# The last query rows' scores of a head pair as four 64x64 products, with the decay bias added outside the array

## The chip, the cores and the metric

The kernel runs on one core of one Trainium2 chip. The metric is device time in microseconds of one execution. PE is TensorE (the matrix engine; PEld its weight loads), DVE is VectorE, ACT is ScalarE, POOL is GpSimd, and SP is the engine whose queue issues most transfers.

## The reference

Attention over 4 batches, 8 heads, 576 positions and 64 dimensions, with a causal mask and a decay from the running sum of a gate, and behind it two feed-forward layers of 512 x 2048 x 512 with different activations on all 2304 tokens. The weights arrive as float64; the kernel splits each into two float32r parts and so runs three products for one in the layers.

```python
def _attn_ref(q, k, v, s):
    scale = 1.0 / np.sqrt(D)
    scores = scale * np.matmul(q, k.transpose(0, 1, 3, 2))
    causal = np.triu(np.ones((S, S), dtype=bool), k=1)
    cum = np.cumsum(np.maximum(s, 0.0), axis=-1)
    bias = -(cum[:, :, :, None] - cum[:, :, None, :])
    scores = np.where(causal, -1000000000.0, scores + np.minimum(bias, 0.0))
    scores = scores - np.max(scores, axis=-1, keepdims=True)
    attn = np.exp(scores)
    attn = attn / (np.sum(attn, axis=-1, keepdims=True) + 1e-09)
    return np.matmul(attn, v)
...
x = attention output as [2304, 512]
h = x @ w_in;  x = np.maximum(0.01 * h, h) @ w_out
h = x @ w_in;  x = (np.maximum(h, 0.0) + np.log1p(np.exp(-np.abs(h)))) @ w_out
```

## The kernel before

**Phases.** Attention comes first and lasts to about 250 us; from then on (the main part) the two layers run as one list of steps, in which a first product fills a bank `ps_h` in PSUM (line 143) and second products fill banks `ps_out` (line 709). Part of layer 0 is drawn into the attention phase: the class `Fill` puts six products of 512 columns (half of an `h` or `o` unit, lines 143 and 583) into each step, as soon as the tokens of a batch are there.

**Pairs, units, steps.** Attention treats two heads at a time (a pair, 16 in all). A pair has four units, in this order: the query rows 384 to 511 of each head (512 keys), the *last* unit with the 64 rows behind 512 of both heads (576 keys), rows 256 to 383, and the two tiles of the first 256 rows. The loop runs over steps n, one per unit; it is a pipeline written out by hand, and each engine's queue follows the order of the code. In step n the scores of unit n + 1 are issued to PE, unit n gets its maxima (DVE, line 305, one instruction that scales, masks and reduces, from PSUM to SBUF) and exponentials (ACT, line 319), unit n - 1 its divisors (DVE, 325 and 326) and normalization (POOL, line 330), and unit n - 2 its transposes (PE, lines 338, 342 and 347) and their copies out of PSUM (lines 359 and 361). The products with V (line 378) are issued in the steps i = 0 and i = 2 of the next pair.

**The scores.** Queries and keys lie in SBUF with the two heads of a pair on the two halves of the partitions. A tile of an ordinary unit is, for each head, a float32 product of 64 rows (`Q`, `K`, line 286, each of two passes in the trace) and a second product that adds the decay: `BQ` and `BK` hold the running sums in two float32r parts and rows of ones, so that their product is the difference of sums between key and query. The last unit (line 276) puts both heads' 64 queries side by side as 128 columns of a stationary operand that has zeros where the other head's dimensions are, and runs over each half of the keys with all 128 rows: `Q` times `K`, then `BQ` times `BK`. Pair 0 uses `BQ0` and `BK0`, built in float32 from the first scans, instead.

**PSUM.** In the attention phase one pool has banks by tag: `s0` and `s1` for scores (two each), `t` for transposes (two), `a` for the products with V and the wake-up (one), `m` for the fill (one). When the attention is over, this pool is closed, and two others are opened over the same space: five banks for `ps_out` and three for `ps_h`.

**Transfers.** In step i = 0 of a pair SP issues the next pair's Q and K and the rows of `BQ` and `BK` (five transfers, line 80, from the DRAM tile `bb_d`), in step i = 3 the next pair's V; weights (`rawi`, `rawo`) and stores of layer 0's partial sums lie in between. At the start, Q and K of pair 0 go through ACT's queue.

Of the kernel before, what the change touches and what calls it, by code (L numbers as in the profile page):

```python
# [2 lines left out]

# [27 lines left out]
def attn_moe_moe(ctx, tc, q, k, v, s, w1i, w1o, w2i, w2o, out):  # L31
# [18 lines left out]
    def pool(name, bufs=1, **kw):  # L50
        return tc.tile_pool(name=name, bufs=bufs, **kw)
# [6 lines left out]
    xh = keep.tile([P, KD, NT], F32R, tag="xh", name="xh")  # L58
    xl = keep.tile([P, KD, NT], F32R, tag="xl", name="xl")
    bb_d = dram.tile([B * H, 2, S], F32R, tag="bb_d", name="bb_d")  # L60
    part = dram.tile([B - 1, P, KD, FW], F32, tag="part", name="part")


# [6 lines left out]
    def tick():  # L70
        clock[0] += 1
        for fn, args in todo.pop(clock[0], ()):
            fn(*args)
# [5 lines left out]
    def move(dst, src, queue=nc.sync):  # L79
        queue.dma_start(dst.bitcast(F32), src.bitcast(F32))  # L80
# [72 lines left out]
    def attention(att, ps, fills):  # L153
# [1 line left out]

        ZQ = NB * P + 2 * TL
        own = [[slice(0, NB * P + TL)], [slice(0, NB * P), slice(NB * P + TL, ZQ)]]
        two = lambda nm, shape, dt=F32: [att.tile(shape, dt, tag=f"{nm}{i}", name=f"{nm}{i}") for i in range(2)]  # L160
        Q, K = two("Q", [P, ZQ]), two("K", [P, S])
        BQ, BK = two("BQ", [P, ZQ], F32R), two("BK", [P, S], F32R)
        V = two("V", [P, NB + 1, 2, D])

        PA = att.tile([P, 2, NB, P + TL], F32, tag="PA", name="PA")
# [10 lines left out]
        def blank(i):  # L176

            bq = BQ[i].bitcast(F32)
            nc.gpsimd.memset(bq, 0.0)
            for j in range(2):  # L180
                for c in own[j]:
                    nc.gpsimd.memset(bq[j * D:j * D + 2, c], 1.0)

        def wake(x):

            pt = ps.tile([P, 512], F32, tag="a", name="pt_w", bufs=1)
            for i in range(8):
                nc.tensor.matmul(pt[:, :P], x, x, start=True, stop=True)

        def decay0():  # L190

            pitch = list(s1.ap[0])[0]
            nc.sync.dma_start(
                bass.AP(s1.tensor, s1.offset, [[D * pitch, 2], [1, S]]), bass.AP(s.tensor, s.offset, [[S, 2], [1, S]])
            )
            load(0, "q", nc.scalar)
            nc.sync.dma_start(c0, s.rearrange("b h s -> (b h) s"))
            load(0, "k", nc.scalar)
            nc.vector.memset(one[:, :P], 1.0)
            wake(one[:, :P])  # L200
            nc.vector.memset(one[:, P:], 1.0)
            nc.vector.memset(base, 0.0)
            for j in range(2):
                nc.vector.memset(base[j * D + 32:j * D + 33], -1.0)
            for i in (1, 0):
                nc.vector.memset(BK[i].bitcast(F32), -1.0)
            nc.vector.tensor_scalar(s0[:1], s1[:1], 0.0, 1.0 / scale, op0=ALU.max, op1=ALU.mult)
            for y, x in ((s0[D:D + 1], s1[D:D + 1]), (c0, c0)):
                nc.scalar.activation(y, x, AF.Relu, scale=1.0 / scale)
            nc.vector.tensor_tensor_scan(BK0, one, s0, base, op0=ALU.mult, op1=ALU.add)  # L210
            nc.scalar.activation(BQ0[32:33, :S], BK0[:1], AF.Copy)
            n = 0
            for c, queue in zip(own[1], (nc.vector, nc.gpsimd)):
                m = n + c.stop - c.start
                queue.tensor_copy(BQ0[D + 32:D + 33, c], BK0[D:D + 1, n:m])
                n = m

        hi, lo = one[:BH], c0

# [4 lines left out]
        def parts():  # L224
            nc.vector.tensor_tensor(lo.bitcast(F32R), c1, hi, op=ALU.subtract)
            for e, x in enumerate((hi, lo)):
                nc.sync.dma_start(bb_d[:, e, :].bitcast(F32), x)

        def zeros():
            nc.gpsimd.memset(PZ[TL:], 0.0)  # L230
# [2 lines left out]
            b, hp = divmod(p, NPAIR)  # L233
            return b, slice(2 * hp, 2 * hp + 2)

        def load(p, nm, queue=nc.sync):
            if p < NP:
                t, x = {"q": (Q, q), "k": (K, k), "v": (V, v)}[nm]
                queue.dma_start(t[p % 2], x[p])

        def rows(p):

            if p < NP:
                b, hs = heads(p)
                for j in range(2):
                    h, r = b * H + hs.start + j, j * D
                    move(BK[p % 2][r:r + 2], bb_d[h])
                    n = 0
                    for c in own[j]:
                        m = n + c.stop - c.start  # L250
                        move(BQ[p % 2][r + 32:r + 34, c], bb_d[h, :, n:m])
                        n = m


        class Unit:
            def __init__(self, p, ts):
                self.p, self.ts = p, ts
                self.last = not ts
                o = 0
                self.subs = []  # L260
                for t in ts:
                    self.subs.append((t, slice(o, o + (t + 1) * P)))
                    o += (t + 1) * P
                self.W = S // 2 if self.last else o
                self.n = 1 if self.last else 2 * len(ts)

            def scores(self):
                i = self.p % 2
                bq, bk = (BQ[i], BK[i]) if self.p else (BQ0, BK0)
                ops = (Q[i], K[i]), (bq, bk)  # L270
                self.ps = [ps.tile([P, 512], F32, tag=f"s{j}", name="pt_s", bufs=2) for j in range(2)]
                if self.last:

                    for j, pt in enumerate(self.ps):
                        for x, y in ops:
                            nc.tensor.matmul(  # L276
                                pt[:, :self.W], x[:, NB * P:], y[:, j * self.W:(j + 1) * self.W],
                                start=x is Q[i], stop=x is bq,
                            )
# [14 lines left out]
            def maxima(self, j):  # L294
                if j == 0:
# [2 lines left out]
                    if self.last:  # L298
                        self.sc = view(self.sc, 0, [self.W, 2], [1, self.W])
                w = slice(0, self.W)  # L300
                todo = [(w, (mask[:, w], maskl)[j], j)] if self.last else [
                    (c, mask[:, (NB - 1 - t) * P:], j * len(self.subs) + i) for i, (t, c) in enumerate(self.subs)
                ]
                for c, m, e in todo:
# [117 lines left out]
            blank(i)  # L422
        decay()
        fill.step(-2)
        load(1, "q")
        load(1, "k")
        fill.step(-1)
# [11 lines left out]
        for n in range(len(units) + 3):  # L439
# [11 lines left out]
            if u2:  # L451
                u2.transpose(0)
            if i == 0:
                if p:
                    load(p + 1, "q")
                    load(p + 1, "k")
                    rows(p + 1)
            tick()
            if n == len(units):
                fill.free = [("m", 1), ("s0", 2), ("s1", 2)]  # L460
# [133 lines left out]
            mm(range(G // 2))  # L594
            self.rest = rest

    with pool("psA", bufs=2, space=PSUM) as psA:
        fills = []

        def make():  # L600
            fills.append(Fill(psA))
            return fills[0]

        with pool("att") as att:
            attention(att, psA, make)
        fill = fills[0]
        while fill.units or fill.rest or todo:
            fill.run()
            tick()
        fill.stack.close()  # L610

    wpools.append(ctx.enter_context(pool("wpool1", bufs=2)))
    for nm in "io":
# [6 lines left out]

    gpool = ctx.enter_context(pool("gpool", bufs=4, side="right"))
    tpool = ctx.enter_context(pool("tpool", bufs=2, side="right"))
    ps_o = ctx.enter_context(pool("ps_o", bufs=5, space=PSUM))
    ps_h = ctx.enter_context(pool("ps_h", bufs=3, space=PSUM))

    chunks = [(0, 512), (512, 512), (1024, NT - 2048), (NT - 1024, 512), (NT - 512, 512)]
    n0 = (B - 1) * FW
# [64 lines left out]
    def out_mm(n):  # L692
# [5 lines left out]

        for i in range(n_out):
            if f == 0:  # L700
                outs[i] = ps_o.tile([P, 512], F32, tag="o", name="ps_out")
        for i in range(n_out):
            sl = slice(i * P, (i + 1) * P)
            if layer == 0:
# [42 lines left out]
    for n, (layer, g, c, is_first, is_last, f) in enumerate(steps):  # L747
        N = c[1]
        cols = slice(c[0], c[0] + N)
        ps = ps_h.tile([P, 512], F32, tag="h", name="ps_h")  # L750
        h_mm(ps[:, :N], layer, g * G + f, xh[:, :, cols], xl[:, :, cols])
        tick()
        settle()
        act1(n, layer, N, ps)
        for fn, w in sorted(plan.pop(n, ()), key=lambda x: (split_w, load_w, load_acc).index(x[0])):
            fn(*w)
        if n >= LAG:
            out_mm(n - LAG)
# [11 lines left out]
def lay_out(name, a):  # L770
# [9 lines left out]
    if name == "v":  # L780
# [1 line left out]
        r[:, :, :n] = a[:, :, :n * P].reshape(-1, 2, n, P, D).transpose(0, 3, 2, 1, 4)  # L782
        r[:, :tl, n] = a[:, :, n * P:].transpose(0, 2, 1, 3)
        return r
    r = np.zeros((B * H // 2, 2, D, S + (tl if name == "q" else 0)), a.dtype)
    r[..., :S] = a.transpose(0, 1, 3, 2)
    if name == "q":
        r[:, 1, :, S:] = r[:, 1, :, n * P:S]
        r[:, 1, :, n * P:S] = 0
    return r.reshape(-1, 2 * D, r.shape[-1])  # L790


# [18 lines left out]
```

## Time and profile before

| | us |
|---|---|
| median of 3 runs | 986.3 |
| the three runs | 985.24, 986.3, 1078.37 |
| the profiled execution | 985.13 |
| its span from the first to the last instruction | 983.4 |
| PE busy in it | 973.2 |
| DVE busy in it | 529.2 |

The run of 1078.37 stands apart from the others and is not compared with anything here. The span is 1.7 us shorter than the profiled execution's own time; times inside the trace count from the span's start.

### The profile page before, as it was taken

The numbers are of one execution on the slowest core, as the hardware profiler recorded it, in microseconds if no ns is written. First come the engines' busy times: TensorE is split into PE (matmuls) and PEld (weight loads), VectorE is DVE, ScalarE is ACT, GpSimd is POOL, SyncE is SP. The second block draws the span as 40 slices with busy tenths as digits, with TensorE's granted clock in tenths as the row PEclk, the third lists the DMA queues.
The fourth block names the chain that finished last, engine by engine and source line by source line (L and its number), as shares of the span: only waits on it lengthen the run. The fifth ranks groups of instructions, "written<-read, shape, count | busy, mean of one in ns | idle before, by whom it ended". The sixth has DMA issues, their size and how long they took to land.

```text
span 983.4 us, 14578 instructions
## 1 busy us (share of the span) xinstructions
PE 973.2 (99%) x5226; PEld 797.1 (81%) x5226; DVE 529.2 (54%) x1139; ACT 537.6 (55%) x1119; POOL 568.5 (58%) x553
## 2 busy tenths in 40 slices
PE   8999999999999999999999999999999999999998
PEld 5767777777898888888888888888888888888886
DVE  7976666555121322232226347767587858764434
ACT  6887667656454333334335456776656555654452
POOL 7766456444264455345535546777777777874554
PEclk9999999999999999999999999999999999999999
DMA  6322331310540111011101210112011101100202
GB/s 200 123 102 81 125 122 63 111 52 25 178 134 22 52 56 43 22 48 60 43 22 44 65 43 22 43 44 64 23 44 43 59 27 44 44 1 1 86 22 86
DMA packets 35239, 61.20 MB, mean 62 GB/s; under 512 B 2566, under 2 KB 19718, under 8 KB 35168
## 3 DMA queue, kind: packets, MB, share of 16 engines
q1 hardware_dynamic: 34736, 59.53, 18.4%
q8 instruction: 41, 0.67, 0.3%
q10 hardware_dynamic: 432, 0.75, 0.2%
q14 instruction: 30, 0.25, 0.1%
HBM read 52.26 MB, written 8.01 MB: 61 GB/s over the span
## 4 chain that ended last, share of the span: by engine, by line
PE 95%; DVE 2%; ACT 1%; POOL 1%; issue 0%; DMA 0%; DVEq 0%; ACTq 0%; POOLq 0%
PE ps_h L143 40%; PE ps_out L709 37%; PE pt_v L378 4%; PE pt_s L286 4%; PE pt_t L347 3%; PE ps_o L583 3%; PE pt_s L276 2%; PE pt_t L342 1%; POOL sc L330 1%; ACT sc L319 1%; DVE sc L305 0%; DMA sc<-in_s 0%; POOL wm L121 0%; DVE acc L724 0%; DVE wm L118 0%
## 5 line engine op out<-in xcount | busy, mean ns | idle before, releaser
L149 POOL TENSOR_TENSOR gl<-gf,gh 128x512 fp32r<-128x512 f32 (+2 forms) x148 | 183.1, 1237 | 151.3 <-ACT gh L148 141.7
L143 PE MATMUL ps_h<-xh,wih 128*128 128x512 f32 (+2 forms) x640 | 237.7, 371 | 0.7 <-ACT o L587 0.7
L143 PE MATMUL ps_h<-xh,wil 128*128 128x512 f32 (+2 forms) x640 | 235.7, 368 | 0.0
L143 PE MATMUL ps_h<-xl,wih 128*128 128x512 f32 (+2 forms) x640 | 235.7, 368 | 0.0
L724 DVE TENSOR_TENSOR acc<-ps_out,acc 128x512 f32<-128x512 f32 (+1 forms) x115 | 73.8, 658 | 164.1 <-PE ps_out L709 164.1
L674 POOL TENSOR_TENSOR t<-e,t 128x512 f32<-128x512 f32 (+1 forms) x80 | 112.3, 1404 | 72.1 <-DVE t L673 71.3
L330 POOL TENSOR_SCALAR sc<-sc,st 128x512 f32<-128x512 f32 (+4 forms) x160 | 87.6, 560 | 96.7 <-DVE st L326 83.5
L143 PEld LDWEIGHTS ps_h<-xh,wih 128*128 128x128 f32 x640 | 120.6, 188 | 20.4 <-ACT o L587 1.2
L143 PEld LDWEIGHTS ps_h<-xh,wil 128*128 128x128 f32 x640 | 120.5, 188 | 19.6
L143 PEld LDWEIGHTS ps_h<-xl,wih 128*128 128x128 f32 x640 | 120.7, 189 | 19.1
L658 ACT ACTIVATE gf<-ps_h 128x512 f32<-128x512 f32 (+2 forms) x68 | 37.2, 547 | 178.1 <-PE ps_h L143 174.1
L148 ACT ACTIVATE gh<-gf 128x512 fp32r<-128x512 f32 (+2 forms) x148 | 86.1, 581 | 49.2 <-DVE gf L684 48.5
L709 PE MATMUL ps_out<-woh,gl 128*128 128x512 f32 x288 | 112.4, 390 | 0.0
L709 PE MATMUL ps_out<-woh,gh 128*128 128x512 f32 x288 | 112.3, 390 | 0.0
L709 PE MATMUL ps_out<-wol,gh 128*128 128x512 f32 x288 | 112.3, 390 | 0.0
L121 POOL TENSOR_TENSOR wm<-wm,wt 128x512 int32<-128x512 int32 x64 | 84.9, 1327 | 30.7 <-DVE wm L118 30.7
L319 ACT ACTIVATE sc<-sc,st 128x512 f32<-128x512 f32 (+2 forms) x144 | 83.5, 585 | 29.4 <-DVE st L325 22.8
L709 PE MATMUL ps_out<-gh,wol 128*128 128x512 f32 (+2 forms) x272 | 99.1, 364 | 0.0
L709 PE MATMUL ps_out<-gh,woh 128*128 128x512 f32 (+2 forms) x272 | 99.1, 364 | 0.0
L709 PE MATMUL ps_out<-gl,woh 128*128 128x512 f32 (+2 forms) x272 | 99.0, 364 | 0.0
L673 DVE TENSOR_SCALAR t<-e 128x512 f32<-128x512 f32 (+1 forms) x80 | 44.3, 553 | 98.4 <-ACT e L664 98.4
L112 DVE TENSOR_SCALAR wm<-wm 128x512 f32<-128x512 f32 x64 | 38.3, 599 | 95.6 <-ACT wm L106 95.4
(107 smaller groups left out, 1704.9 us busy)
## 6 DMA issues: line engine op xcount, KB each, us to landing
rawi<-in_moe_w_in SPq DMA_DIRECT2D x32, 512.0 KB
rawo<-in_moe_w_out SPq DMA_DIRECT2D x32, 512.0 KB
V<-in_v SPq DMA_DIRECT2D x16, 320.0 KB
Q<-in_q SPq DMA_DIRECT2D x15, 320.0 KB
out<-acc SPq DMA_DIRECT2D x17, 256.0 KB
K<-in_k SPq DMA_DIRECT2D x15, 288.0 KB
part<-o SPq DMA_DIRECT2D x12, 256.0 KB
acc<-part SPq DMA_DIRECT2D x3, 1024.0 KB
```

Of the source, the lines that this page charges most:

```text
L121: nc.gpsimd.tensor_tensor(m, m, t, op=ALU.add)
L143: nc.tensor.matmul(ps, a, b, start=kk == 0 and n == 0, stop=kk == KD - 1 and n == 2)
L148: nc.scalar.activation(gh, gf, AF.Copy)
L149: nc.gpsimd.tensor_tensor(gl, gf, gh.bitcast(F32), op=ALU.subtract)
L286: nc.tensor.matmul(self.ps[j][:, c], x[r, t * P:(t + 1) * P], y[r, :(t + 1) * P], start=x is Q[i], stop=x is bq,)
L319: nc.scalar.activation(x, x, AF.Exp, scale=-1.0, bias=self.stat(0, e), accum_out=self.stat(1, e))
L330: nc.gpsimd.tensor_scalar(x, x, self.stat(2, e), 1.0, op0=ALU.mult, op1=ALU.mult)
L378: nc.tensor.matmul(pt[j * D:(j + 1) * D, o:o + w], V[p % 2][:, c, j, :], x[:, j, :], start=m == 0 or (not last and m == 1), stop=m == len( ...
L673: nc.vector.tensor_scalar(t, e, 1.0, -1.0, op0=ALU.add, op1=ALU.add)
L674: nc.gpsimd.tensor_tensor(t, e, t, op=ALU.subtract)
L709: nc.tensor.matmul(ps, a, b, start=f == 0 and m == 0, stop=f == G - 1 and m == 2)
L724: nc.vector.tensor_tensor(d[..., x], o[..., x], d[..., x], op=ALU.add)
```

## The change

It touches four places.

1. The last unit's scores. For each head there is a 64-row stationary block of 64 queries, once against the first and once against the second half of its keys: four products of 64 x 64 with 288 columns each (float32). They lie on the four quadrants of the array. To that end Q gets 64 columns more that hold the other head's last queries (before, these held the second head's queries with zeros around), and K gets 288 columns more with the other head's keys, so that a pair's K load is 432 KB instead of 288. Only pair 0 adds its decay by a full-size product as before.
2. The decay of the last unit for pairs 1 to 15. The running sums go to a DRAM tile `c_d` as well. In step i = 2 of a pair, SP loads the next pair's sums into a tile `M`, each head's row into 64 partitions, and one value per partition (the query's own sum) into a further column. In step i = 0 of the next pair, behind the first unit's `maxima(0)`, DVE subtracts that column from the 576 others and adds the causal mask to the last 64 (`bias`). The last unit's maxima take `M` in place of the mask. The rows of `BQ` shrink from five to four transfers a pair, and `BQ` and `BK` from 640 and 576 columns to 512.
3. `wake` issues 12 products of 128 columns instead of 8. The second part of K of pair 0 goes through SP's queue behind the first weight load.
4. The PSUM pool of the attention phase stays open to the end. In the main part `ps_h` takes its banks in turn from `t`, `t`, `a`, and `ps_out` from `m`, `s0`, `s0`, `s1`, `s1`.

```diff
+    c_d = dram.tile([B * H, S], F32, tag="c_d", name="c_d")
...
-        ZQ = NB * P + 2 * TL
-        own = [[slice(0, NB * P + TL)], [slice(0, NB * P), slice(NB * P + TL, ZQ)]]
+        SB, SH = NB * P, S // 2
+        ZQ, ZK = S + TL, S + SH
...
-        Q, K = two("Q", [P, ZQ]), two("K", [P, S])
-        BQ, BK = two("BQ", [P, ZQ], F32R), two("BK", [P, S], F32R)
+        Q, K = two("Q", [P, ZQ]), two("K", [P, ZK])
+        BQ, BK = two("BQ", [P, SB], F32R), two("BK", [P, SB], F32R)
+        M = att.tile([P, S + 32], F32, tag="M", name="M")
...
-            for i in range(8):
+            for i in range(12):
                 nc.tensor.matmul(pt[:, :P], x, x, start=True, stop=True)
...
-            load(0, "k", nc.scalar)
+            load(0, "k", nc.scalar, slice(0, S))
...
             for e, x in enumerate((hi, lo)):
                 nc.sync.dma_start(bb_d[:, e, :].bitcast(F32), x)
+            nc.sync.dma_start(c_d, c1)
...
-                    move(BK[p % 2][r:r + 2], bb_d[h])
-                    n = 0
-                    for c in own[j]:
-                        m = n + c.stop - c.start
-                        move(BQ[p % 2][r + 32:r + 34, c], bb_d[h, :, n:m])
-                        n = m
+                    move(BK[p % 2][r:r + 2], bb_d[h, :, :SB])
+                    move(BQ[p % 2][r + 32:r + 34], bb_d[h, :, :SB])
+
+        def decays(p):
+
+            if p < NP:
+                o = c_d.offset + p * 2 * S
+                nc.sync.dma_start(M[:, :S], bass.AP(c_d.tensor, o, [[S, 2], [0, D], [1, S]]))
+                nc.sync.dma_start(M[:, S:S + 1], bass.AP(c_d.tensor, o + SB, [[S, 2], [1, TL], [1, 1]]))
+
+        def bias(p):
+            if 0 < p < NP:
+                nc.vector.tensor_scalar(M[:, :S], M[:, :S], M[:, S:S + 1], None, op0=ALU.subtract)
+                nc.vector.tensor_tensor(M[:, SB:S], M[:, SB:S], maskl[:, SH - TL:], op=ALU.add)
...
-                    for j, pt in enumerate(self.ps):
-                        for x, y in ops:
+                    for e in range(2):
+                        for j, pt in enumerate(self.ps):
+                            r, o = (slice(h * D, (h + 1) * D) for h in (j, j ^ e))
+                            x, y = (S, S) if e else (SB, j * SH)
                             nc.tensor.matmul(
-                                pt[:, :self.W], x[:, NB * P:], y[:, j * self.W:(j + 1) * self.W],
-                                start=x is Q[i], stop=x is bq,
+                                pt[o, :SH], Q[i][r, x:x + TL], K[i][r, y:y + SH], start=True, stop=self.p > 0
+                            )
+                    if not self.p:
+                        for j, pt in enumerate(self.ps):
+                            nc.tensor.matmul(
+                                pt[:, :SH], bq[:, SB:], bk[:, j * SH:(j + 1) * SH], start=False, stop=True
                             )
...
-                todo = [(w, (mask[:, w], maskl)[j], j)] if self.last else [
+                ml = (mask[:, w], maskl)[j] if not self.p else M[:, j * SH:(j + 1) * SH]
+                todo = [(w, ml, j)] if self.last else [
...
         decay()
         fill.step(-2)
+        load(0, "k", nc.sync, slice(S, None))
         load(1, "q")
...
             if i == 0:
+                bias(p)
                 if p:
                     load(p + 1, "q")
                     load(p + 1, "k")
                     rows(p + 1)
+            elif i == 2:
+                decays(p + 1)
...
-    with pool("psA", bufs=2, space=PSUM) as psA:
+    psA = ctx.enter_context(pool("psA", bufs=2, space=PSUM))
...
-    ps_o = ctx.enter_context(pool("ps_o", bufs=5, space=PSUM))
-    ps_h = ctx.enter_context(pool("ps_h", bufs=3, space=PSUM))
+    banks = {
+        "ps_h": cycle((("t", 2), ("t", 2), ("a", 1))),
+        "ps_out": cycle((("m", 1), ("s0", 2), ("s0", 2), ("s1", 2), ("s1", 2))),
+    }
+
+    def bank(nm):
+        tag, bufs = next(banks[nm])
+        return psA.tile([P, 512], F32, tag=tag, name=nm, bufs=bufs)
...
-                outs[i] = ps_o.tile([P, 512], F32, tag="o", name="ps_out")
+                outs[i] = bank("ps_out")
...
-        ps = ps_h.tile([P, 512], F32, tag="h", name="ps_h")
+        ps = bank("ps_h")
```

## Rows read from the trace of the kernel before

**Rows 1.** The page: busy time by engine, and 40 slices of granted clock.

```profile
PE 973.2 (99%) x5226; PEld 797.1 (81%) x5226; DVE 529.2 (54%) x1139; ACT 537.6 (55%) x1119; POOL 568.5 (58%) x553
...
PEclk9999999999999999999999999999999999999999
```

**Rows 2.** The waits of PE: who waited for whom, us in all, times, longest.

```profile
PE pt_w L188 <- DVE V L199: 1.0, 1, 1.0
...
PE ps_h L143 <- ACT o L587: 0.7, 1, 0.7
```

**Rows 3.** Stretches, one per pair: busy time of PE, PEld, DVE, ACT, POOL; clock; DMA.

```profile
18.15:30.79 12.64, 11.89 (x92) 8.27 (x92) 11.55 (x38) 10.01 (x30) 10.26 (x14) 1.00 0.29 89
30.79:41.56 10.77, 10.77 (x93) 7.93 (x92) 10.29 (x40) 9.98 (x30) 8.59 (x13) 1.00 0.42 143
41.56:52.34 10.78, 10.78 (x94) 7.96 (x92) 9.46 (x34) 9.34 (x27) 7.43 (x13) 1.00 0.41 134
52.34:66.25 13.91, 13.43 (x99) 9.29 (x98) 12.23 (x44) 11.30 (x36) 9.62 (x14) 1.00 0.31 116
...
113.89:130.22 16.33, 16.33 (x118) 12.26 (x116) 9.65 (x37) 10.29 (x31) 8.05 (x12) 1.00 0.40 125
```

**Rows 4.** PE in order of time (start, us), the last unit's scores of pair 8.

```profile
113.78 0.27 PE L338 MATMUL pt_t<-ident,sc 128*64 128x128 f32 x1
113.89 0.65 PE L276 MATMUL pt_s<-K,Q 128*128 128x288 f32 x2
...
114.51 0.65 PE L276 MATMUL pt_s<-K,Q 128*128 128x288 f32 x2
...
115.13 0.49 PE L347 MATMUL pt_t<-ident,sc 128*128 128x128 f32 x3
```

**Rows 5.** PE in order of time: V's products and an ordinary unit's scores.

```profile
100.92 1.52 PE L378 MATMUL pt_v<-PA,V 128*64 128x192 f32 x16
102.27 0.28 PE L378 MATMUL pt_v<-PZ,V 128*64 128x64 f32 x4
...
105.28 0.49 PE L347 MATMUL pt_t<-ident,sc 128*128 128x128 f32 x3
105.70 0.70 PE L286 MATMUL pt_s<-K,Q 64*128 64x256 f32 x4
...
106.35 0.39 PE L286 MATMUL pt_s<-K,Q 64*128 64x128 f32 x4
106.49 0.31 PE L286 MATMUL pt_s<-BK,BQ 64*128 64x128 f32 x2
106.73 0.66 PE L347 MATMUL pt_t<-ident,sc 128*128 128x128 f32 x4
```

**Rows 6.** Lines 112 and 310 on DVE: shortest, median and longest of each, ns.

```profile
L112 DVE TENSOR_SCALAR wm<-wm x64: 410/428/1365, 10.9 to 873.0; 128x512 f32<-128x512 f32 x64
...
L310 DVE TENSOR_TENSOR st<-st x16: 158/612/1307, 12.7 to 233.0; 128x1 f32<-128x1 f32 x16
```

**Rows 7.** DVE in order of time: ends of maxima in pairs 2 and 3.

```profile
35.70 0.08 DVE L305 DVE_READ_ACCUMULATOR2_ANT st<- 128x1 f32 x1
...
43.06 0.07 DVE L305 DVE_READ_ACCUMULATOR2_ANT st<- 128x1 f32 x1
```

**Rows 8.** PE in order of time: the start.

```profile
1.04 3.48 PE L188 MATMUL pt_w<-V 128*128 128x128 f32 x16 [1.04 <-DVE V L199]
...
5.20 1.13 PE L286 MATMUL pt_s<-K,Q 64*128 64x512 f32 x4 [0.68 <-DMA K<-in_k]
...
7.85 0.75 PE L276 MATMUL pt_s<-K,Q 128*128 128x288 f32 x2
...
11.77 0.70 PE L286 MATMUL pt_s<-K,Q 64*128 64x256 f32 x2 [0.23 <-DVE st L305]
```

**Rows 9.** PE in order of time: the seam between attention and main part.

```profile
254.46 0.39 PE L583 MATMUL ps_o<-gh,wol 128*128 128x512 f32 x1
255.58 0.44 PE L143 MATMUL ps_h<-xh,wih 128*128 128x384 f32 x1 [0.74 <-ACT o L587]
```

More of the change, by code (lines that the diff above doesn't have):

```diff
@@ L2 @@
 from contextlib import ExitStack
+from itertools import cycle
 import concourse.bass as bass
@@ L180, in blank @@
             for j in range(2):
-                for c in own[j]:
-                    nc.gpsimd.memset(bq[j * D:j * D + 2, c], 1.0)
+                nc.gpsimd.memset(bq[j * D:j * D + 2], 1.0)
         def wake(x):
             pt = ps.tile([P, 512], F32, tag="a", name="pt_w", bufs=1)
-            for i in range(8):
+            for i in range(12):
                 nc.tensor.matmul(pt[:, :P], x, x, start=True, stop=True)
@@ L211, in decay0 @@
             nc.scalar.activation(BQ0[32:33, :S], BK0[:1], AF.Copy)
-            n = 0
-            for c, queue in zip(own[1], (nc.vector, nc.gpsimd)):
-                m = n + c.stop - c.start
-                queue.tensor_copy(BQ0[D + 32:D + 33, c], BK0[D:D + 1, n:m])
-                n = m
+            for c, n, queue in ((slice(0, SB), 0, nc.vector), (slice(S, ZQ), SB, nc.gpsimd)):
+                queue.tensor_copy(BQ0[D + 32:D + 33, c], BK0[D:D + 1, n:n + c.stop - c.start])
         hi, lo = one[:BH], c0
@@ L234, in heads, with load @@
             return b, slice(2 * hp, 2 * hp + 2)
-        def load(p, nm, queue=nc.sync):
+        def load(p, nm, queue=nc.sync, c=slice(None)):
             if p < NP:
                 t, x = {"q": (Q, q), "k": (K, k), "v": (V, v)}[nm]
-                queue.dma_start(t[p % 2], x[p])
+                queue.dma_start(t[p % 2][:, c], x[p, :, c])
         def rows(p):
@@ L246, in rows @@
                     h, r = b * H + hs.start + j, j * D
-                    move(BK[p % 2][r:r + 2], bb_d[h])
-                    n = 0
-                    for c in own[j]:
-                        m = n + c.stop - c.start
-                        move(BQ[p % 2][r + 32:r + 34, c], bb_d[h, :, n:m])
-                        n = m
+                    move(BK[p % 2][r:r + 2], bb_d[h, :, :SB])
[9 more added lines that the diff above has]
+                nc.vector.tensor_tensor(M[:, SB:S], M[:, SB:S], maskl[:, SH - TL:], op=ALU.add)
         class Unit:
@@ L263, in __init__ @@
                     o += (t + 1) * P
-                self.W = S // 2 if self.last else o
+                self.W = SH if self.last else o
                 self.n = 1 if self.last else 2 * len(ts)
@@ L595, in o, with make @@
             self.rest = rest
-    with pool("psA", bufs=2, space=PSUM) as psA:
[L598 to L610, printed above, removed]
+    psA = ctx.enter_context(pool("psA", bufs=2, space=PSUM))
+    fills = []
+    def make():
+        fills.append(Fill(psA))
+        return fills[0]
+    with pool("att") as att:
+        attention(att, psA, make)
+    fill = fills[0]
+    while fill.units or fill.rest or todo:
+        fill.run()
+        tick()
+    fill.stack.close()
     wpools.append(ctx.enter_context(pool("wpool1", bufs=2)))
@@ L784, in lay_out @@
         return r
-    r = np.zeros((B * H // 2, 2, D, S + (tl if name == "q" else 0)), a.dtype)
-    r[..., :S] = a.transpose(0, 1, 3, 2)
+    a = a.transpose(0, 1, 3, 2)
     if name == "q":
-        r[:, 1, :, S:] = r[:, 1, :, n * P:S]
-        r[:, 1, :, n * P:S] = 0
-    return r.reshape(-1, 2 * D, r.shape[-1])
+        more = a[:, ::-1, :, n * P:]
+    else:
+        more = np.stack([a[:, 1, :, :S // 2], a[:, 0, :, S // 2:]], 1)
+    return np.concatenate([a, more], -1).reshape(B * H // 2, 2 * D, -1)
 def kernel(**inputs):
```

## The prediction

> **What bounds the kernel now.** I read the page's engine table first: TensorE (PE) is busy 973.2 of 983.4 us and VectorE (DVE) 529.2 [rows 1]. Since a busy PE need not be at its peak, the second view is PE's list of waits: its eleven lines sum to 6 us for the whole span, none over 1.0 [rows 2]. The third cuts the attention phase into pairs of heads, numbered from 0, from one last unit's first score product to the next; the rows are pairs 1 to 4 and 8 [rows 3]. Pairs 2 and 3 take 10.77 and 10.78 us although their DVE load differs (10.29 and 9.46), and PE is busy in all of it: a period that stays while the others' load changes is PE's own instruction stream. In pair 8 it is so too, with the fill's products in between. So a nanosecond taken from PE is a nanosecond of the end, as long as nobody else becomes late. In pairs 1 to 4 that is near: DVE is idle 1.09, 0.48, 1.32 and 1.68 us of each [rows 3]. In pair 8, which stands for 5 to 15, it is idle for 6.7. The main part behind 255 us is PE alone, and the change leaves its arithmetic as it is.
>
> **The last unit's scores.** Before, in a steady pair, they hold PE from 113.89 to 115.13: 1.24 us [rows 4]. Of that, an fp32 product is two passes: two of them last 0.65 together and one 0.41, so they start 0.24 apart. Per half of the keys that is 0.48 for q times k, and 0.14 is left of 0.62 for the decay product.
> After, each of the four 64x64 products again has two passes of 288 columns. That PE runs products on two row halves at once is seen at line 286: four passes of 256 columns (0.21 each at the same rate) and two decay passes of 256 (0.12 each) take 0.65 to the start of the next tile, 105.70 to 106.35 [rows 5]; in turn they would need 1.08. Two column halves run at once at line 378: sixteen passes of 192 columns take 1.35 us up to the next group [rows 5], where 192 columns are 0.16 a pass by the above, so that one after another they would need 2.56. Both halvings together are not in this trace. Bounds: 0.48 for all four at once, 1.92 for one after another; I take 0.48, because each axis alone shows full overlap.
> Added to it are the changes of shape. Entry: three transposes ahead of a 64-row product take 0.42 (105.28 to 105.70) [rows 5], where a transpose ahead of a full-size product takes 0.11 [rows 4], so 0.09 is extra. First weights: 1.35 less 8 x 0.16 is 0.05 to 0.07; I take 0.05. Exit: from the last 64-row pass (128 columns of one pass, 0.06 by the 0.14 for 288) to the transpose behind it are 0.24 (106.49 to 106.73), 0.18 extra; and the weights behind it I put at 0.05 again. With 0.02 for staggered starts: 0.09 + 0.05 + 0.48 + 0.02 + 0.18 + 0.05 = 0.87. **The gain is 1.24 - 0.87 = 0.37 us per pair**, half of what the vanished passes suggest. Ends: 0.69 (all shape costs but weights and stagger vanish) and -1.07 (eight passes in turn with all of them).
> The Trainium skill speaks against the change here: "TensorEngine Tiling (Array Packing)", Tiling Modes, Key Properties, says that a change of tiling mode drains TensorE. The 0.09 and 0.18 bear it out; by the rule both stay and the sum is mine, without it the sum would be that of the first rival.
>
> In pairs 5 to 15, eleven of them, PE sets the period: 11 x 0.37 = **4.1 us gained**.
>
> **The bias on VectorE.** Per pair from the second on: one subtraction with a per-partition operand on 128x576 and one addition on 128x64. The subtraction's nearest row is the clamp of weights (L112, 128x512): 0.41 at least, 0.43 median [rows 6], so 0.47 for 576; the addition's is L310 (two SBUF inputs, one column): 0.16 at least, 0.61 median, 1.31 at most [rows 6]. Bounds 0.6 to 1.8, and never a gain, since nothing leaves DVE; I take the medians, 0.47 + 0.61 = 1.1. It stands between the two maxima of the pair's first unit, so behind it on DVE wait the second maximum, its exponential, and the copies of transposes out of PSUM. In pairs 5 to 15 the idle DVE hides it. If that cover were gone, each pair would pay up to 1.1. In pairs 1 to 4 it is compared with DVE's idle time and PE's gain: pair 1 11.55 + 1.1 = 12.65 against 12.64, some of its idle time being waits that stay, +0.4; pair 2 11.39 against 10.77, +0.6; pair 3 10.56 against 10.78, -0.2; pair 4 13.33 against 13.91, so PE's 0.37 is kept, -0.4. **Together +0.4**, between -1.5 (DVE never late, 4 x 0.37) and +4.4 (never hidden). The maxima read M where they read the mask; that changes nothing, as L305 reads a tile of that size already.
>
> **Transfers.** Per pair SP issues two more (M, 288 KB, and 128 single values), two rows less go into BQ for the last queries, and K grows by half. M has one buffer: its load waits for the last unit's second maximum, done at 35.70 in pair 2, and the next pair's bias wants it at 43.06 [rows 7]: 7.4 us; in pairs 16.33 long instead of 10.77, about 11.2. Pair 0's Q and K (608 KB together) let the first scores go 5.20 after the program's start [rows 8], so half as much lands in less than that; hidden. Behind M's load on SP stand the next weight, V and store issues; before it waits only for DVE work already done, so they move little.
>
> **Start.** Four more wake-up products: the sixteen passes end at 4.52, PE then idles 0.68 for K [rows 8]; eight more passes at 0.11 are 0.85, so 0.2 late. The granted clock is 1.00 (2.4 GHz) in all 40 slices [rows 1], so nothing is to be had from them. The second part of K is needed at about 7.9 and is issued behind 512 KB of weights: 0 to 1 us late. Against it, PE waits for DVE at 11.77 anyway [rows 8], which absorbs delays and also swallows what pair 0 would save. **+0.2**, from -0.2 to +1.
>
> **The seam.** The last ps_o product starts at 254.46 and needs 0.23 for 512 columns at the one-pass rate above, yet ps_h begins at 255.58 because the new PSUM pools wait for the last copy out of the old one [rows 2, 9]. Now ps_h takes banks t and a, which were copied out earlier. **0.9 us gained**; what comes next is PE's own stream. The rotation has three and five banks as before, so the main part keeps its time. If the copy of the last o is wanted by something else there, 0.
>
> **Sum.** The profiled execution took 985.1 (span 983.4 and 1.7 around it); two other runs took 985.2 and 986.3. -4.1 + 0.4 + 0.2 - 0.9 = -4.4: 980.7, and as the median lies a little higher than the profiled run, I say 981. About 2%, 20 us, is what a measurement can tell from no change here. All last units together are 16 x 1.24 = 20 us, so even scores that cost nothing would hardly get there.
>
> **Rivals.**
> First, changes of shape cost nothing: 0.55 per unit, 0.69 x 11 = 7.6 gained, 985.1 - 7.6 - 0.9 + 0.6 = 977. Against it stand the gaps in [rows 5]; for it, that transposes and 64-wide products might share a shape.
> Second, VectorE takes over in the early pairs because additions wait for GpSimd (L310's slow cases): bias 1.8, pairs 1 to 4 pay 0.7 + 1.3 + 0.5 + 0.1 = 2.6, giving 983; with 2 us more of knock-on on exponentials and banks, 985. For it: DVE idle 0.48 in pair 2. Against it: pairs 3 and 4 have more than twice that to catch up in.
> Third, the change does not do what it says: the four products share the array two at a time only. Then 2 x 0.48 + 0.39 = 1.35, a loss of 0.11 per pair: 985.1 + 1.2 + 0.4 + 0.2 - 0.9 = 986. In turn, 1.07 lost in 15 pairs: 985.1 + 16.1 - 0.7 = 1001. Against both: each axis alone overlaps.
> Fourth, ending slower: M lands late. DVE then stands at the bias with everything behind it. It decides from 7.4 us after issue in pairs 1 to 4 and from 11.2 later. A landing of 12 us costs 4 x 4.6 + 11 x 0.8 = 27, less the 4.4 of the sum: 1008. For it: each row of M is fetched from the same DRAM line 64 times and 128 values of four bytes come on their own. Against it: 608 KB within 5.2 us [rows 8].
>
> **Chances.** Forecast 0.55 (979 to 983 by its bounds), first rival 0.14, second 0.14, third 0.09 and 0.04, fourth 0.04. The range 976 to 988 leaves out the last two and a little of the ends. Faster by over 2%: 0.01, by what I can't price; slower by over 2%: 0.03, most of the fourth; within 2%: 0.96.
>
> **What would show it.** In the new score lines: four first passes within 0.03 us, the unit 0.8 to 0.9 us from its first pass's entry to the transpose, steady pairs of 15.96 instead of 16.33. DVE: subtraction 0.4 to 0.6, addition 0.2 to 1.3; pair 2 at 11 us or more with DVE without gaps. No wait of DVE for M. ps_h straight behind ps_o. It is wrong if the first passes start 0.24 apart, if steady pairs don't shrink, or if DVE waits for a DMA at the bias.

## The result and the profile after

The changed kernel takes 992.56 us (median of 6 runs, 991.8 to 995.09) against 986.35 for the kernel before: 1.0072 times as long, with an interval from 1.0057 to 1.0088. It is 6 us slower where 5 us less were forecast, and outside the range of 976 to 988. The profiled execution took 995.09, its span 993.3 us; it is the longest of the six, so the rows below show a loss of 9.9 us where the medians differ by 6.2.

The page of the changed kernel, its busy times and granted clock:

```profile
PE 976.8 (98%) x5268; PEld 790.5 (80%) x5268; DVE 543.0 (55%) x1169; ACT 537.0 (54%) x1119; POOL 570.8 (57%) x551
...
PEclk9799999999999999999999999999999999999999
```

PE does 3.6 us more than in [rows 1] in a span 9.9 us longer: most of the loss is PE standing idle, and one slice, the second, has a lower clock. The stretches of the pairs say where. As in [rows 3] each runs from one last unit's first score product to the next; these are pairs 1 to 4 and 8 of the changed kernel (columns: length; busy time and count of PE, PEld, DVE, ACT, POOL; granted clock; DMA share; GB/s):

```profile
18.47:37.25 18.78, 14.17 (x95) 9.19 (x94) 11.47 (x42) 10.30 (x32) 11.43 (x15) 0.82 0.40 100
37.25:51.55 14.30, 12.83 (x94) 8.40 (x93) 11.72 (x40) 9.66 (x28) 8.33 (x13) 0.88 0.57 125
51.55:64.89 13.34, 11.85 (x94) 7.72 (x93) 10.56 (x36) 9.07 (x24) 6.73 (x12) 1.00 0.59 175
64.89:80.91 16.02, 14.05 (x101) 8.88 (x100) 12.90 (x46) 11.24 (x36) 9.98 (x14) 1.00 0.42 98
128.31:144.40 16.09, 16.09 (x119) 11.40 (x118) 9.88 (x39) 10.30 (x31) 8.19 (x12) 1.00 0.50 149
```

Beside [rows 3], pairs 1 to 4 are 6.1, 3.5, 2.6 and 2.1 us longer, and PE is idle in each for 1.5 to 4.6 us; no engine is full (PE, the busiest, for 75 to 90%). Pair 5 loses another 0.5 (16.84 against 16.33). From then on the sign turns: pair 8 is 0.24 shorter, pairs 6 to 14 together 3.5, and from pair 15's first score to the end 1.7 are gained. With 0.3 lost at the start, 14.8 - 3.5 - 1.7 + 0.3 makes the 9.9 by which the span is longer. So the change has a small gain per pair, as forecast, and a large loss within pairs 1 to 5.

Who ends last in that loss is told by the chain of waits of the changed kernel from 15 to 60 us (start, us, what):

```profile
15.12 0.57 SPq L254
...
15.74 9.95 DMA M<-c_d
...
25.79 0.53 DVE M L259
...
26.34 0.23 DVE M L260
26.56 0.60 DVE sc L320
...
29.53 0.36 DVE sc L320
29.93 0.51 SPq L254
...
30.48 9.37 DMA M<-c_d
...
39.94 1.67 DVE M L259
...
44.86 0.52 SPq L254
...
45.42 9.10 DMA M<-c_d
...
54.62 1.30 DVE M L259
```

This is a loop: M's transfer is issued, lands 9 to 10 us later (the chain counts from the issue of the single values, L255; from that of the rows, L254, it is 9.6 to 10.6), the subtraction and addition follow, then the next unit's maxima read M (L320, second half at 29.53), and only then is M free for the next load at 29.93. Issues stand at 29.93, 44.86 and 59.16: 14 to 15 us a turn, against the 10.8 us in which pairs 2 and 3 ran before. No product of PE is in it. The list of waits of the changed kernel agrees (who waited for whom: us in all, times, longest; DVE's row is for 0 to 260 us):

```profile
DVE M L259 <- DMA M<-c_d: 12.5, 8, 4.6
```

```profile
PE pt_s L300 <- DVE st L320: 8.1, 5, 3.7
```

DVE waits at the bias, and PE for the maxima queued behind it. Compared with the list in [rows 2], where no wait of PE was over 1.0, this is new.

How M moves is seen in the DMA share of two short stretches, and PE's clock in two others (columns as above):

```profile
15.80:17.50 1.70, 1.25 (x8) 0.41 (x7) 1.67 (x8) 1.70 (x5) 1.26 (x2) 1.00 0.86 268
17.90:20.90 3.00, 1.78 (x16) 0.93 (x15) 3.00 (x10) 2.04 (x9) 2.64 (x3) 1.00 0.14 55
26.40:33.10 6.70, 5.87 (x25) 4.19 (x26) 5.81 (x22) 5.13 (x13) 3.67 (x5) 0.50 0.08 27
43.40:46.80 3.40, 3.40 (x16) 2.38 (x16) 3.03 (x14) 2.97 (x8) 1.36 (x2) 0.50 0.05 15
```

From 17.9 to 20.9 us the share is 0.14 of 16 DMA engines, which is 2.2 engines, at 55 GB/s; just before, with other transfers in flight, it was 0.86 at 268. M's source pattern `[[S, 2], [0, D], [1, S]]` has an outermost dimension of 2. The trace also keeps every packet that the DMA engines moved, with its size, and here M's 128 rows are packets of 2304 bytes: they move from 17.78 to 23.79 us, on average 2.0 under way at a time. Over all 15 loads they take 6.0 to 7.5 us each.

The last two rows are a follow-on: after PE had stood waiting, its granted clock was 0.50 (the 1.2 GHz level) for 6.7 and for 3.4 us. Those stretches lie beside the chain shown above, which holds no product.

### The profile page after: what moved, and what is told of

Same layout as the page of the kernel before. It is cut to its first block, busy times and chain, and to the rows that moved or that the text cites. A ratio compares the mean times of both kernels' runs of the same rounds, so it can differ in the third digit from the quotient of the medians.

```text
span 993.3 us, 14734 instructions
## 1 busy us (share of the span) xinstructions
PE 976.8 (98%) x5268; PEld 790.5 (80%) x5268; DVE 543.0 (55%) x1169; ACT 537.0 (54%) x1119; POOL 570.8 (57%) x551
## 4 chain that ended last, share of the span: by engine, by line
PE 91%; DMA 5%; DVE 2%; ACT 1%; SPq 0%; issue 0%; DVEq 0%
PE ps_h L145 40%; PE ps_out L734 36%; DMA M<-c_d 5%; PE pt_s L300 4%; PE pt_v L393 3%; PE ps_o L602 3%; PE pt_t L362 3%; PE pt_s L286 1%; DVE M L259 1%; PE pt_t L357 1%; DVE sc L320 1%; PE pt_w L190 1%; ACT sc L334 1%; DMA bb_d<-PA 0%; SPq L254 0%; DVE acc L749 0%
## 5 line engine op out<-in xcount | busy, mean ns | idle before, releaser
L345 POOL TENSOR_SCALAR sc<-sc,st 128x512 f32<-128x512 f32 (+4 forms) x160 | 90.0, 573 | 106.3 <-DVE st L341 95.6
```

Source lines behind the costliest of these rows:

```text
L345: nc.gpsimd.tensor_scalar(x, x, self.stat(2, e), 1.0, op0=ALU.mult, op1=ALU.mult)
```

## The experiments

Each was timed beside runs of the kernel before on the same chip, and the ratios are to that kernel. The theory after the result: M's transfer runs on few DMA engines because its pattern's outermost dimension is 2. Rivals: its 128 single values are the slow part; M's single buffer is the fault, however fast the load; the score products or VectorE's two operations cost more than forecast.

**M by head.** Same bytes, two transfers of 64 rows, whose outermost dimension is 64.

```diff
-                nc.sync.dma_start(M[:, :S], bass.AP(c_d.tensor, o, [[S, 2], [0, D], [1, S]]))
-                nc.sync.dma_start(M[:, S:S + 1], bass.AP(c_d.tensor, o + SB, [[S, 2], [1, TL], [1, 1]]))
+                for j in range(2):
+                    m = M[j * D:(j + 1) * D]
+                    nc.sync.dma_start(m[:, :S], bass.AP(c_d.tensor, o + j * S, [[0, D], [1, S]]))
+                    nc.sync.dma_start(m[:, S:S + 1], bass.AP(c_d.tensor, o + j * S + SB, [[1, TL], [1, 1]]))
```

> The changed kernel with M loaded by two transfers of 64 rows (and the column by two of 64 values) instead of one with an outer dimension of 2. Theory A (the outer dimension of 2 puts the 128 rows on two of the 16 DMA engines, so that M takes 9 to 10 us from issue to landing): DMA share in the stretch of M's rows well above 0.14, landing after 4 to 5 us, no or little wait of VectorE for M, 981 to 984 us. Rival B (the 128 four-byte values are slow): landing and time stay, 991 to 993. Rival C (64 rows from one DRAM line are slow): the same, 991 to 993. Rival D (the work on VectorE itself is the loss, not the wait): 990 to 993.

980.91 (the ratio to the kernel before is 0.9956, its interval 0.9944 to 0.9969; likewise below). DVE no longer waits for M. Stretches of this kernel (columns as above), pairs 2 and 3:

```profile
31.18:42.28 11.10, 11.06 (x94) 7.52 (x94) 10.30 (x43) 9.63 (x29) 8.74 (x13) 1.00 0.54 168
42.28:53.35 11.07, 10.95 (x94) 7.54 (x93) 9.64 (x38) 9.41 (x28) 7.72 (x13) 1.00 0.48 163
```

M's 128 rows now move from 16.99 to 18.74 us, 9.7 under way at a time, and take 1.8 to 3.0 us over all loads. PE is busy again in nearly all of each pair, and the clock is 1.00. One transfer's pattern is worth 12 us, the whole loss and the forecast's gain with it.

**Two buffers for M**, each loaded a pair earlier, pattern unchanged.

```diff
+        Ms = two("M", [P, S + 32])
...
-                decays(p + 1)
+                if not p:
+                    decays(1)
+                decays(p + 2)
```

> The changed kernel with two M buffers, each loaded one pair earlier; the transfer keeps its form. If the wait for M is the loss (A, B and C alike): landing still 9 us or more, but no wait of VectorE for M, pairs 2 and 3 at 10.5 to 11.5 us, 981 to 984 us. Rival D (VectorE's added work): pairs 1 to 4 keep 2 to 3 us of the loss each, 988 to 992.

988.28 (1.0032, 1.0018 to 1.0045): missed. DVE waits for M once only, 4.3 us in pair 1 (which still takes 18.72), so the loop is gone; yet pair 2 still takes 14.73. There the weights are late. The chain of waits of this kernel shows the transfer, and ACT in order of time the first use of these weights (start, busy, wait in brackets):

```profile
33.69 10.10 DMA rawi<-in_moe_w_in
```

```profile
43.81 0.66 ACT L108 ACTIVATE wm<-rawi 128x512 f32<-128x512 f32 x1 [2.26 <-DMA rawi<-in_moe_w_in]
```

So the narrow transfer has two victims: who reads M, and whoever's transfer is queued behind it. A second buffer helps the first only.

**No column.** The single values are loaded for pair 1 only.

```diff
+                if p == 1:
                     nc.sync.dma_start(M[:, S:S + 1], bass.AP(c_d.tensor, o + SB, [[S, 2], [1, TL], [1, 1]]))
```

> The changed kernel with the column of own sums loaded for pair 1 only: later pairs subtract pair 1's column, so their last rows get a wrong constant. Theory A: the rows still come on two engines, landing shorter by the column's 1 to 2 us only, 986 to 991 us. Rival B (the four-byte values are the slow part): landing 4 to 5 us, 981 to 984.

990.14 (1.005, 1.0034 to 1.0066): 2.4 us under the change's median, though the intervals of the two ratios overlap. M's 576 columns still land late. This line of its chain of waits is pair 3's load, which has rows alone:

```profile
42.47 8.95 DMA M<-c_d
```

From the rows' issue that is 8.95 us where the change had 9.66 for the same pair, so the rival of the single values falls as the main cause. They do have a cost of their own, at the issue behind them; it is told under "Why the prediction was wrong".

**Quads without M.** The kernel before with the four 64x64 products; its decay stays a product, for which both halves' sums are kept.

```diff
+                                 pt[o, :SH], Q[i][r, x:x + TL], K[i][r, y:y + SH], start=True, stop=False
...
+                            pt[:, :SH], bq[:, SB:], bk[:, j * SH:(j + 1) * SH], start=False, stop=True
```

> The kernel before with the four 64x64 products alone (with the longer K and Q); the decay stays a full-size product, there is no M, 8 wake-up products and the old PSUM pools. If the products do what the traces show (0.65 us plus changes of shape, against 0.97 for the two full ones): 0.1 to 0.25 us gained per pair, 982 to 985.5 us. If the larger K load or the change of shape costs elsewhere: 986 to 990.

983.89 (0.9984, 0.9974 to 0.9994), steady pairs 16.20 instead of 16.34. PE in order of time in pair 8:

```profile
113.60 0.71 PE L279 MATMUL pt_s<-K,Q 64*64 64x288 f32 x8
114.24 0.54 PE L283 MATMUL pt_s<-BK,BQ 128*128 128x288 f32 x2
114.62 0.49 PE L353 MATMUL pt_t<-ident,sc 128*128 128x128 f32 x3
```

The unit holds PE for 1.02 instead of 1.24 us, and 0.14 of that arrives per steady pair (entry takes 0.09 more, as below). Pairs 2 and 3 take 10.81 and 10.67, so there nothing arrives. The products are not what slows the change.

**Outermost dimension of 2 again, by head.** Two copies of the sums in DRAM stand for the first half's and the second half's rows, so that each of the two transfers per pair has an outermost dimension of 2.

```diff
-                    nc.sync.dma_start(m[:, :S], bass.AP(c_d.tensor, o + j * S, [[0, D], [1, S]]))
+                    nc.sync.dma_start(m[:, :S], bass.AP(c_d.tensor, o + j * S, [[B * H * S, 2], [0, D // 2], [1, S]]))
```

> The run x1_m_by_head with one thing changed back: each head's transfer has an outer dimension of 2 again (two copies of the sums in DRAM, 32 rows from each), with the same number of transfers and bytes. Theory A (the outer dimension sets over how many DMA engines a transfer spreads): the stretch of M's rows has a DMA share near 0.14 again, waits of VectorE for M return, 987 to 993 us. If splitting by head alone, or something else of the form, was the cure: 980 to 983.

1000.97 (1.0157, 1.0142 to 1.0173). The loss is back, though each row is now fetched half as often from one address; it is even larger than that of the change. In its list of waits and chain:

```profile
DVE M L262 <- DMA M<-c_d: 17.6, 9, 4.0
```

```profile
16.35 10.43 DMA M<-c_d
...
33.22 10.87 DMA M<-c_d
```

Pairs 1 to 3 take 19.67, 16.25 and 16.81 in the profiled execution, the longest of the five (1006.64). The DMA share expected near 0.14 couldn't be read, since other transfers ran beside (0.61 to 0.93); but by the packets M's rows again move 2.0 at a time in the first load. That it is slower than the change itself was not expected: its 128 rows take 7.4 to 10.0 us a load, 125 ns a row on average, where the change took 6.0 to 7.5 and 104, and the last of M's transfers is the fourth issue instead of the second. Why a row takes longer, no run shows.

**Outermost dimension of 8, by head**: eight copies, `[[B * H * S, 8], [0, D // 8], [1, S]]`.

> The run x9_outer_2 with eight copies of the sums in DRAM and eight rows from each, so an outer dimension of 8 in place of 2, everything else the same (one larger store of the sums at the start). Theory A (the outer dimension sets the number of DMA engines, here 8): near x1_m_by_head, 981 to 984 us, little or no wait of VectorE for M. If copies in DRAM as such made that run slow: 995 to 1001.

981.15 (0.9951, 0.9935 to 0.9968), and DVE never waits for M. Together: outermost 2 gives 992.6 and 1001.0, outermost 8 and 64 give 981.2 and 980.9. The time can't tell 8 from 64, since both are hidden, but the rows' own move tells 2 from more: 6.0 to 7.5 and 7.4 to 10.0 us at 2, 2.4 to 3.7 at 8, 1.8 to 3.0 at 64. This is what a count of engines should show. That the same DRAM row is read many times is ruled out: with 64 as the outermost dimension it is read 64 times, and fast.

**The narrow transfer that nobody reads.** The kernel before, with the change's two loads of M in step i = 2 and, for them, its store of the sums to `c_d`.

```diff
+            elif i == 2:
+                decays(p + 1)
```

> The kernel before, scores and all, with the two transfers into M as the change makes them; nothing reads M and its load waits for nobody. If the only loss is that VectorE waits for M: 985 to 986 us. If transfers queued behind M's rows on the same two engines come late as well (the weights of x2_two_m landed 10.1 us after issue): 987 to 992 us, with waits of ACT for weights or of PE for K, Q or V.

990.0 (1.004, 1.0027 to 1.0054). Nobody waits for M, and still pair 2 goes from 10.77 to 14.66, because weights come late: the chain of waits of this kernel, and ACT in order of time:

```profile
28.12 9.66 DMA rawi<-in_moe_w_in
```

```profile
37.80 0.66 ACT L107 ACTIVATE wm<-rawi 128x512 f32<-128x512 f32 x1 [2.96 <-DMA rawi<-in_moe_w_in]
```

512 KB of weights behind M land after 9.66 us. So a good part of the loss (4 to 5 us) needs no reader of M. The late weights aren't all of it. PE in order of time, in this kernel and in the kernel before, runs the same products up to 37.0 us; then come:

```profile
39.53 1.73 PE L357 MATMUL pt_t<-ident,sc 128*128 128x128 f32 x8 [2.22 <-ACT PB L369]
41.19 2.48 PE L388 MATMUL pt_v<-PB,V 128*64 128x128 f32 x16
```

```profile
37.20 1.09 PE L347 MATMUL pt_t<-ident,sc 128*128 128x128 f32 x8
38.22 1.52 PE L378 MATMUL pt_v<-PB,V 128*64 128x128 f32 x16
```

They start 2.33 us later, and from there to the next scores (43.60 against 39.67) take 4.07 instead of 2.47, at a granted clock of 0.50 from 39.77 to 43.18. So of the 3.9 us that pair 2 loses 2.3 are the weights and 1.6 the halved clock behind the wait.

**VectorE's two operations left out**, on top of M by head.

```diff
-                nc.vector.tensor_scalar(M[:, :S], M[:, :S], M[:, S:S + 1], None, op0=ALU.subtract)
-                nc.vector.tensor_tensor(M[:, SB:S], M[:, SB:S], maskl[:, SH - TL:], op=ALU.add)
```

> The run x1_m_by_head without VectorE's subtraction and addition: the last rows then have neither their own sum subtracted nor the causal mask. If these two set the 12.90, 11.11, 11.07 and 14.61 us of pairs 1 to 4 there (rival two of the prediction): pairs 2 and 3 at 10.3 to 10.4, all in all 1.5 to 3 us less than that run, 978 to 979.5. If the loss in these pairs comes from the larger loads: within 0.7 us of it.

979.77 (0.9943, 0.993 to 0.9955), 1.1 us less than with them, between the two expectations. Pairs 1 to 4 take 12.68, 10.78, 10.69 and 14.03 instead of 12.90, 11.11, 11.07 and 14.61. Pairs 2 and 3 were to fall to 10.3 or 10.4 and don't, so PE isn't the only limit there. Part of the difference isn't VectorE's: in the profiles of two other kernels with both operations, outermost 8 and M by head with eight wake-up products, pair 4 takes 14.02 and 14.04, as it does here.

**The subtraction alone left out**, with the column. A query's own sum is the same for all keys of its row, so the softmax cancels it.

```diff
-                    nc.sync.dma_start(m[:, S:S + 1], bass.AP(c_d.tensor, o + j * S + SB, [[1, TL], [1, 1]]))
...
-                nc.vector.tensor_scalar(M[:, :S], M[:, :S], M[:, S:S + 1], None, op0=ALU.subtract)
```

> The run x1_m_by_head without the subtraction of the query's own sum and without the column for it: a constant per row falls out of the softmax, so the result is the same. VectorE keeps the addition on 64 columns only. If VectorE's work is what pairs 1 to 4 lose: 0.8 to 2.2 us less, 978.8 to 980.2; else within 0.5 us of 980.9.

979.6 (0.9941, 0.9929 to 0.9954), the same as without both. Stretches of its pairs 2 and 3:

```profile
30.94:41.71 10.77, 10.73 (x94) 7.21 (x93) 10.22 (x41) 9.85 (x30) 8.60 (x13) 1.00 0.60 173
41.71:52.40 10.69, 10.57 (x95) 7.11 (x94) 9.48 (x35) 9.17 (x25) 7.40 (x13) 1.00 0.61 189
```

**Eight wake-up products instead of twelve**, on M by head (first) and on the kernel without subtraction (second).

```diff
-            for i in range(12):
+            for i in range(8):
```

> The run x1_m_by_head with 8 wake-up products. By the prediction's term the four more cost 0.2 us: 0.2 to 0.4 us less, 980.5 to 981. If they help the start: 0.3 to 1 us more.

> The run x8_no_subtract with 8 wake-up products, the shortest version by the runs so far. If the four more cost nothing: 979.3 to 979.9 us, as that run; by the prediction's 0.2: 979.2 to 979.5.

980.93 (0.9956, 0.9943 to 0.9968) and 979.54 (0.9937, 0.9924 to 0.9949): no difference to 980.91 and 979.6. The second, level with the kernel that keeps twelve, is the fastest run here, by its ratio 6.2 us under the kernel before.

**The kept PSUM pool alone**, in the kernel before.

```diff
-    with pool("psA", bufs=2, space=PSUM) as psA:
+    psA = ctx.enter_context(pool("psA", bufs=2, space=PSUM))
```

> The kernel before with the kept PSUM pool alone. By the prediction's term the gap between the last ps_o and the first ps_h goes: 0.9 us less than before, 984.2 to 984.6 us, ps_h straight behind ps_o. If something else holds the first ps_h there, or the banks' new order costs in the main part: 985 or more.

984.24 (0.9985, 0.9976 to 0.9994). The profiled spans differ by 0.9 (982.5 against 983.4), and the trace shows that 0.9 at the seam, as below. The median of the kernel before beside it is 986.31, 2 us more, but beside most other runs it was 985.1 to 985.3, so the rest can't be put down to the pool.

## Why the prediction was wrong

**What failed is the step headed "Transfers"**: "half as much lands in less than that; hidden". It sized M's landing by Q's and K's bytes [rows 8], and M moves fewer bytes on fewer engines. Measured: 9 to 10 us from issue to landing, against the 7.4 us that pairs 2 and 3 leave [rows 7]. The fourth rival named this mechanism, with DVE standing at the bias, and its point of decision held: the four pairs with 7.4 us lose, steady pairs with 11.2 don't. (Pair 5 loses another 0.5, and in pairs 8 to 10 DVE still waits for M, 1.79 us at most, which its idle time hides.) Its chance of 0.04 was too low and its reasons were wrong: neither the single values (no column: 2.4 us of 12) nor the repeated fetch from one row (64 times at outermost 64, hidden) is the cause.

This could have been worked out before the run. The Trainium skill, "DMA: Bandwidth & Descriptors", in the section on why a DMA increments its semaphore by 16 and not by 1, says that a transfer runs on the largest number of engines up to 16 that divides the slowest dimension of both patterns, and its later row on using all 16 engines says that an outermost dimension under 16 holds the whole transfer to at most that many. By it M had 2, the outermost 8 had 8 and M by head 16; the share of 0.14, the 2.0 packets at a time and the rows' times at 2, 8 and 64 agree.

**"Behind M's load ... they move little" failed as well**: 512 KB of weights behind it land after 10 us (two buffers, idle M). The packets of the run without the column show why. Behind M's rows for pair 2, 448 of the weights' 512 packets move from 30.57 to 33.17 us, beside M's rows. The other 64 are an eighth, as 2 engines are of 16, and move only from 36.76 to 38.48, when M's last row is done (36.80). In the changed kernel SP itself is held up too, in order of time; its issue of V behind M's two took 4.14 us, whereas with M by head it took 0.53:

```profile
15.12 0.57 SPq L254 DMA_DIRECT2D M<-c_d  x1
15.74 0.50 SPq L255 DMA_DIRECT2D M<-c_d  x1
16.28 4.14 SPq L239 DMA_DIRECT2D V<-in_v  x1
```

```profile
17.04 0.53 SPq L239 DMA_DIRECT2D V<-in_v  x1
```

This hold-up belongs to the single values: without the column, the issue of weights behind M's rows for pairs 2 to 4 takes 0.41 to 0.47, where the changed kernel took 3.41, 3.56 and 0.60; behind pair 1's load, which still has the column, V's issue takes 4.31.

**The scores** were right. In pair 8 of the changed kernel, PE in order of time:

```profile
128.11 0.27 PE L353 MATMUL pt_t<-ident,sc 128*64 128x128 f32 x1
128.31 0.72 PE L286 MATMUL pt_s<-K,Q 64*64 64x288 f32 x8
128.96 0.55 PE L362 MATMUL pt_t<-ident,sc 128*128 128x128 f32 x3
```

Eight passes take 0.65 us to the transpose behind them, changes of shape included, where [rows 4] had 1.24; the four first passes start within 0.02 us of each other, the second ones 0.29 later. Entry is 0.20 against 0.11, the 0.09 that was forecast. From the last transpose ahead to the product behind the three transposes the steady pairs now take 1.15 us where they took 1.59 (pairs 7 and 8, the one shown, 1.31). So the unit comes to about 0.80 and the steady pairs to 15.9 to 16.1: up to 0.43 a pair gained (0.37 forecast). The third rival is dead, and the first, at 0.69, too.

**VectorE.** The two operations of the changed kernel (shortest, median, longest, ns):

```profile
L259 DVE TENSOR_SCALAR M<-M x15: 506/520/1657, 25.8 to 239.7; 128x576 f32<-128x576 f32 x15
L260 DVE TENSOR_TENSOR M<-M,maskl x15: 226/381/383, 26.3 to 240.2; 128x64 f32<-128x64 f32 x15
```

0.90 a pair where 1.1 was said. What they cost was under-sized: without them pairs 1 to 4 take 48.18 us together; with M by head it was 49.69, and in the profiles of outermost 8 and of eight wake-up products 49.14 and 49.19. So "together +0.4" measures +1.0 to +1.6 (against 48.10 in [rows 3]), within its bounds. The second rival's direction is in that, but not its reason: the additions of up to 1.31 us did not come, 0.383 being the longest.

Under it lies a premise that failed. "PE's own instruction stream" was to set the period of pairs 2 and 3, so that PE's 0.37 would be gained there too. With the four 64x64 products alone they take 10.81 and 10.67, without DVE's operations 10.78 and 10.69, against 10.77 and 10.78 before: almost nothing arrives. What else holds them is open.

**The start** lost 0.3 (0.2 forecast), but the wake-up products can't be shown to be its cause. They run to 6.25 in the changed kernel and the first score follows; with M by head the same number ends at 5.48. Of the two kernels without subtraction, the one with twelve starts its first score at 5.97 and the one with eight at 5.70, and both reach pair 0's last unit at 7.89. In the profiles of the kernels with twelve, pair 1's first score stands anywhere from 18.16 to 19.11 (18.15 in the kernel before), so 0.3 is within what one profile differs from the next.

```profile
1.04 5.21 PE L190 MATMUL pt_w<-V 128*128 128x128 f32 x24 [1.04 <-DVE V L201]
...
6.19 1.13 PE L300 MATMUL pt_s<-K,Q 64*128 64x512 f32 x4
```

**The seam** was right: ps_h starts 0.23 behind the start of the last ps_o where [rows 9] had 1.12, 0.89 gained (0.9 forecast).

```profile
265.60 0.39 PE L602 MATMUL ps_o<-gh,wol 128*128 128x512 f32 x1
265.83 0.33 PE L145 MATMUL ps_h<-xh,wih 128*128 128x384 f32 x1
```

**With the transfer spread, the sum comes out.** M by head takes 980.91 where 981 was forecast. By its stretches, pairs 5 to 15 give 4.6 (4.1 said), pairs 1 to 4 cost 1.6 (0.4), the start 0.1 (0.2), the seam gives 0.9 (0.9), and the main part 0.3. That it fits so closely is luck in part: the cost of pairs 1 to 4 was put 1.2 too low, and the gains of pairs 5 to 15 and of the main part 0.8 too low.

Open: how much of pairs 1 and 2 of the changed kernel the halved clock costs by itself, since PE's slow stretches lie there beside a chain that has no PE in it (with the idle M it is 1.6 us); why pairs 2 and 3 stay at 10.7 without VectorE's operations; and why a row takes longer with outermost 2 by head.

## What to carry to other kernels

Price a transfer by one with the same outermost dimensions on both sides, not by one of more bytes: spread over few engines, 288 KB took 9 to 10 us here, while 608 KB in another pattern were there within 5.2 [rows 8]. With a single buffer, add up issue, landing, use and the last reader, and compare the loop with the shortest period in the kernel, not the usual one. Then look at what stands behind the transfer on its queue, which is late even when nobody waits for the transfer itself. And count a wait of PE twice if its clock falls behind it: with the idle M, 2.3 us of waiting brought 1.6 us at the halved clock.

## What was not expected of the hardware

A broadcast of 128 rows of 2304 bytes whose source has an outermost dimension of 2 moved at 55 GB/s with a DMA share of 0.14, and landed 9 to 10 us after its issue; weights issued behind it landed after 9.7 to 10.1 us. The issue behind its 128 single values took 4.14 us on SP instead of 0.53, and without them 0.41 to 0.47. Four 64x64 fp32 products on the four quadrants ran fully side by side: starts within 0.02 us, eight passes of 288 columns in 0.65 us. And after waits of up to 3.7 us PE's granted clock fell to 0.50 (the 1.2 GHz level) for 6.7 and 3.4 us, in a kernel that otherwise shows 1.00 up to its last microsecond.
